# The last 96 gate and up columns as one token-major product, GpSimd's phi in quarters, another order of the first loads, and new due times

## The chip, the cores and the metric

The kernel runs on one core of one Trainium2 chip. Its metric is the device time in microseconds (us). A kernel's time is the median of its runs; a profile is one further look at a single execution.

## The reference

Two layers of the same kind are applied to a sequence x of 2048 tokens with 512 features, in bf16. Each layer has an attention part A and a gated part B, and both add to x:

```python
def A(x):                                    # x is layer-normed
    q, k, v = heads(x @ wqkv)                # 32 heads of 16
    pq, pk  = q @ w_phi[h], k @ w_phi[h]     # 16x16 for each head
    phi_q = concat(softmax(pq), softmax(-pq))
    phi_k = concat(softmax(pk), softmax(-pk))
    kv, z = phi_k.T @ v, sum(phi_k)          # over all tokens
    return ((phi_q @ kv) / (phi_q . z + 1e-6)) @ wo

def B(x):                                    # x is layer-normed
    gate, up = x @ W_gate, x @ W_up          # 512 -> 1376
    return (relu(gate) * up) @ W_down        # 1376 -> 512

x = x + A(norm(x)); x = x + B(norm(x)); x = x + A(norm(x)); x = x + B(norm(x))
```

The attention is linear: the sums kv and z over all tokens must be complete before the first query can be answered, in each layer.

## The kernel before

The 2048 tokens are 16 tiles of 128. All of x stays in SBUF (X, four chunks of four tiles). Weights are folded at the start: Wk2 and Wq2 are wk and wq times the block-diagonal form Wblk of w_phi (`fold`, line 500, fed by turned weights, line 492).

Each layer has these stages:

- **Keys** (`Keys.tile`), for each tile: K (line 555) and V (561) on TensorE; two exponentials ek on ScalarE (558); their sums over 16 features on VectorE (566); a logarithm and an exponential as a reciprocal on ScalarE (569, 571); the product phiK (575) on GpSimd in layer 0, on VectorE in layer 1 (the last tile of layer 0 and the last two of layer 1 are halved between both); and the sums kv and z (590) on TensorE, which accumulate in three PSUM banks.
- **Queries** (`queries`, 627 and 631), for a chunk of four tiles: Q on TensorE, then two exponentials Eq on ScalarE.
- **Attention** (`attend`), for each tile: Eq times R (645), where R is made of the finished sums (607, 614); ScalarE evacuates to N and DS (652); six VectorE operations up to o (658 to 670); a transpose to oT; wo (674); and the addition to X (678).
- **MLP** (`mlp`), for a block of one, two or four tiles (`BLOCKS`): statistics (524, 525), centring (693), a transpose to xnTB, gate and up (717), relu and copy on ScalarE (729, 732), their product hT on VectorE (735), down (753), and the addition to X (760), after which the next layer's norm of that tile, or its store, can begin.

In gate and up the weights are the stationary operand. The 1376 columns are ten groups of 128 and one of 96, and a group takes four matmuls for gate and four for up, each as wide as the block has tokens (128, 256 or 512). The result lies feature by feature, as down needs it. `step` groups share a PSUM bank in narrow blocks, and the group of 96 has its own evacuations and product.

Norms are transposed by TensorE (515, with ident) for some tiles at the start and at stage changes, else by a DMA transpose in SyncE's queue (512). SyncE also issues most loads (421) and the stores (814). Before the keys, SyncE loads x0, x1, w_phi (wf) and further x tiles; ScalarE issues four loads, wk and wv in halves, and then loads its table (435). wk lies in the first hT buffer at that time. Eight matmuls on zeros (472) start TensorE's clock.

The order of the work is settled before anything is emitted. Every instruction group is an `Op` with an engine, a cost and a due time. `plan` walks through time and lets, on each engine, the operation with the earliest due time go among those that can start; it knows buffers, a DMA queue with a rate, eight DMA lanes, and a flag `port` that keeps VectorE and GpSimd operations on a shared port apart. The due times are the table `DUE`, one number for each operation. The engines' programs then hold the instructions in that order, with the waits that the data need.

Of the kernel before, what the change touches and what calls it, by code (L numbers as in the profile page):

```python
# [8 lines left out]
P = 128  # L9
D = 512  # L10
H = 32
DH = 16
F = 1376
NB = D // P
NF = 11
T = 16
# [48 lines left out]
LANES = 8  # L65


def plan(ops):
# [14 lines left out]
    while len(order) < len(ops):  # L83
# [9 lines left out]
        for e, cand in open_.items():  # L93
# [14 lines left out]
            if first is None or (best is not None and first >= best[0]):  # L108
                continue
            best = first, min((o for t, o in at if t <= first + 1), key=rank)  # L110
        assert best is not None, "no instruction can go"
        t, o = best
# [5 lines left out]
        if o.move:  # L118
            queue = max(t + 1400, queue) + o.move
            lat = max(lat, queue + 600 - t)  # L120
            lanes = lanes[1:] + [t + lat + HOP["SP"]]
# [75 lines left out]
POOL_PHI = (1930, 1940)  # L197
# [8 lines left out]
class K:  # L206
# [8 lines left out]
PHI = ["POOL"] * 15 + ["BOTH"]  # L215
# [5 lines left out]
    12838, 22903, 21957, 14591, 13091, 13645, 15535, 64723, 20066, 21946, 22404, 37433, 28497, 23438, 37063, 39628,  # L221
    28785, 29551, 44842, 28330, 24305, 34896, 63622, 64383, 20084, 27070, 12367, 25403, 16122, 20963, 16400, 20414,
    28622, 14745, 13296, 0, 20852, 19738, 11034, 1902, 20892, 15574, 21335, 14487, 15440, 22432, 23645, 18853, 17105,
    22553, 28873, 19773, 26092, 25340, 25787, 23828, 13120, 23528, 21785, 24083, 23090, 21952, 20538, 24815, 23457,
    25970, 23550, 31010, 25099, 23275, 18650, 19003, 26038, 17503, 25082, 25647, 15810, 16800, 15591, 12341, 14834,
    14960, 22006, 26736, 27644, 31701, 20249, 19795, 19482, 28729, 28028, 25143, 23422, 23168, 21986, 20764, 21010,
    18380, 22535, 26069, 26704, 26760, 27662, 26937, 23439, 25716, 25111, 22983, 25319, 23584, 22831, 20905, 24972,
    20900, 23792, 31557, 26979, 24090, 26712, 27328, 29633, 36593, 23721, 21790, 27888, 29989, 28308, 24211, 23690,
    16282, 27043, 28746, 63959, 20753, 24108, 22204, 20506, 28938, 31501, 16952, 23241, 24872, 26922, 26823, 26681,
    23442, 21284, 21898, 21956, 23204, 34727, 23722, 25793, 25045, 24516, 28101, 34925, 27683, 29170, 28253, 28875,  # L230
    30193, 28228, 27230, 20124, 19920, 25218, 34824, 20364, 26494, 23600, 22279, 25188, 32338, 24418, 23597, 25625,
    24807, 22909, 26881, 23790, 23537, 27214, 30398, 27170, 29691, 24862, 29838, 30880, 31272, 31170, 24090, 19394,
    24355, 27559, 28096, 28185, 27041, 16432, 19783, 20871, 21413, 25680, 24329, 22590, 23232, 28648, 34644, 25165,
    27573, 28614, 28868, 26952, 25768, 33460, 18665, 20698, 17926, 25363, 24420, 41432, 26543, 26946, 21970, 28607,
    28989, 25096, 31074, 29971, 29937, 25959, 28788, 30567, 21366, 23689, 25468, 26088, 25065, 28026, 32472, 33442,
    31477, 34059, 28202, 31806, 26064, 29854, 28369, 27149, 33755, 29216, 28180, 39321, 29625, 29410, 29759, 29949,
    30883, 29890, 21203, 25098, 24304, 21581, 23455, 24475, 31469, 24994, 27083, 22812, 27946, 25205, 43875, 15559,
    25460, 23347, 27182, 23482, 28342, 27010, 22914, 29784, 25417, 28800, 29241, 25959, 25485, 27617, 28609, 37268,
    25605, 25139, 29044, 33664, 26596, 31241, 22317, 27365, 31505, 25855, 27240, 29739, 29776, 24515, 29496, 27055,
# [115 lines left out]
def kernel(  # L355
# [80 lines left out]
    for t in (2, 3):  # L436
        load_x(t, 1, 3 + t)
    for t in (4, 6):
        load_x(t, 2, 3 + t)
# [413 lines left out]
```

The softmax here doesn't subtract the row's maximum and nothing guards it: scores larger than these inputs give would overflow.

## Time and profile before

| | before |
|---|---|
| median of 5 runs | 399.43 us (398.39 to 400.02) |
| the profiled execution, its own time | 399.67 us |
| its span, from the first to the last instruction | 397.8 us |
| mean granted TensorE clock | 0.996 |
| TensorE (PE) busy | 385.9 us, 2819 matmuls |
| VectorE (DVE) busy | 267.4 us |
| ScalarE (ACT) busy | 258.9 us |
| GpSimd (POOL) busy | 34.2 us |

The span leaves 1.87 us of that execution outside. An engine's busy time is the union of its instructions. A matmul's duration in the profile runs from its start until its results have drained, and consecutive matmuls overlap, so the mean of one is longer than the time from one to the next. PEld are the weight loads, which run beside matmuls.

### The profile page before, as it was taken

What the parts mean: (1) busy time and instruction counts of PE and PEld (TensorE: products, weight loads), DVE (VectorE), ACT (ScalarE), POOL (GpSimd) and SP (SyncE); (2) the same over time, 40 slices, a digit from 0 to 9 for tenths busy, and PEclk for the clock granted to TensorE, in tenths of its full rate; (3) what the DMA queues carried; (4) which work ended last, traced back from release to release, by engine and by line L of the source; (5) the groups of instructions that cost most, each with busy time, mean ns of one, the idle gap of its engine ahead of it and who ended that gap; (6) DMA issues with size and microseconds to landing.
All of it is one profiled execution on the core that took longest, in us unless ns stands there. A gap on an engine that the chain in (4) does not pass through costs nothing.

```text
span 397.8 us, 7594 instructions
## 1 busy us (share of the span) xinstructions
PE 385.9 (97%) x2819; PEld 232.6 (58%) x2819; DVE 267.4 (67%) x657; ACT 258.9 (65%) x694; POOL 34.2 (9%) x24
## 2 busy tenths in 40 slices
PE   6998999999999999999999999999999999999996
PEld 4453555786664444454666755577865444444866
DVE  5999846999999442488882458699997513423323
ACT  4788999986835666536684569998842651660622
POOL 0255980000000000000000003000000000000000
PEclk9899999999999999999999999999999999999999
DMA  7457760125424100130100100013334102001010
GB/s 213 94 138 195 202 172 1 28 55 82 80 28 80 28 0 0 28 67 15 40 16 2 26 0 2 4 34 72 69 73 99 29 0 67 15 1 51 16 41 28
DMA packets 56293, 21.78 MB, mean 55 GB/s; under 512 B 48096, under 2 KB 55232, under 8 KB 56256
## 3 DMA queue, kind: packets, MB, share of 16 engines
q1 hardware_dynamic: 55168, 20.25, 22.8%
q10 hardware_dynamic: 1088, 1.05, 0.8%
q8 instruction: 22, 0.36, 0.4%
q14 instruction: 15, 0.12, 0.1%
HBM read 7.91 MB, written 2.10 MB: 25 GB/s over the span
## 4 chain that ended last, share of the span: by engine, by line
PE 74%; DVE 12%; ACT 4%; issue 2%; DVEq 0%
PE b L717 34%; PE b L753 17%; PE b L561 5%; PE b L555 5%; PE b L674 4%; PE b L627 4%; PE q L590 3%; DVE X L678 2%; ACT Eq L631 2%; DVE bstB L524 2%; DVE pr L667 2%; PE q L645 1%; DVE o L670 1%; ACT N L652 1%; DVE m L662 1%
## 5 line engine op out<-in xcount | busy, mean ns | idle before, releaser
L717 PE MATMUL b<-xnTB,wu 128*128 128x128 bf16 (+4 forms) x660 | 89.7, 279 | 0.1
L717 PE MATMUL b<-xnTB,wg 128*128 128x128 bf16 (+5 forms) x660 | 89.3, 279 | 0.0
L729 ACT ACTIVATE gu<-b 128x512 bf16<-128x512 f32 (+4 forms) x98 | 54.6, 572 | 51.4 <-PE b L717 51.1
L735 DVE TENSOR_TENSOR hT<-gu 128x512 bf16<-128x512 bf16 (+4 forms) x98 | 38.0, 393 | 71.2 <-ACT gu L732 70.8
L753 PE MATMUL b<-wd,hT 128*128 128x512 bf16 (+2 forms) x363 | 83.2, 373 | 0.0
L732 ACT CAST gu<-b 128x512 bf16<-128x512 f32 (+3 forms) x98 | 54.3, 563 | 37.6 <-PE b L717 36.9
L717 PEld LDWEIGHTS <-wu 128*128 128x128 bf16 (+1 forms) x660 | 55.2, 100 | 25.1 <-issue 0.4
L717 PEld LDWEIGHTS <-wg 128*128 128x128 bf16 (+1 forms) x660 | 55.0, 100 | 25.5
L753 PEld LDWEIGHTS <-hT 128*128 128x128 bf16 (+1 forms) x363 | 34.8, 98 | 34.8
L575 POOL TENSOR_TENSOR phiK<-ek,sk 128x1024 bf16<-128x1024 bf16 (+1 forms) x18 | 33.5, 1875 | 213.1 <-ACT sk L571 208.3
L652 ACT CAST N<-q 128x384 bf16<-128x384 f32 (+1 forms) x96 | 48.4, 593 | 2.8 <-PE q L645 2.5
L631 ACT ACTIVATE Eq<-b 128x512 bf16<-128x512 f32 x64 | 40.5, 676 | 7.5 <-PE b L627 7.4
L566 DVE TENSOR_REDUCE sk<-ek 128x64 f32<-128x1024 bf16 x32 | 38.2, 1212 | 10.5 <-ACT ek L558 10.1
L558 ACT ACTIVATE ek<-b 128x512 bf16<-128x512 f32 x64 | 35.7, 615 | 5.4 <-PE b L555 5.2
L760 DVE SCALAR_TENSOR_TENSOR X<-b,rsB,X 128x512 bf16<-128x512 f32 (+1 forms) x33 | 23.1, 727 | 23.2 <-PE b L753 23.2
L561 PE MATMUL b<-wv,xnTA 128*128 128x512 bf16 x128 | 33.2, 387 | 0.7 <-ACT ek L558 0.7
L555 PE MATMUL b<-Wk,xnTA 128*128 128x512 bf16 x128 | 32.4, 381 | 1.3 <-ACT vext L479 1.2
L674 PE MATMUL b<-wo,oT 128*128 128x512 bf16 x128 | 32.2, 379 | 1.4 <-ACT oT L479 0.8
L627 PE MATMUL b<-xnTA,Wq 128*128 128x512 bf16 x128 | 31.5, 379 | 0.3 <-ACT Eq L631 0.3
L652 ACT COPY DS<-q 128x48 f32<-128x48 f32 (+1 forms) x96 | 25.3, 344 | 3.1 <-PE q L645 2.2
L645 PE MATMUL q<-R,Eq 128*128 128x144 bf16 x256 | 25.4, 226 | 0.6 <-ACT N L652 0.6
L645 PEld LDWEIGHTS <-Eq 128*128 128x128 bf16 x256 | 19.2, 98 | 8.2 <-issue 0.9
(63 smaller groups left out, 375.2 us busy)
## 6 DMA issues: line engine op xcount, KB each, us to landing
out_dram<-X SPq DMA_DIRECT2D x15, 128.0 KB, 1.7
X<-in_A_x_dram SPq DMA_DIRECT2D x6, 256.0 KB, 3.5
wg<-in_B_W_gate_dram SPq DMA_DIRECT2D x4, 344.0 KB, 4.3
wu<-in_B_W_up_dram SPq DMA_DIRECT2D x4, 344.0 KB, 3.9
wd<-in_B_W_down_dram SPq DMA_DIRECT2D x5, 256.0 KB, 4.2
hT<-in_A_wqkv_dram ACTq DMA_DIRECT2D x2, 256.0 KB, 3.6
X<-in_A_x_dram SPq DMA_DIRECT2D x4, 128.0 KB, 3.7
wv<-in_A_wqkv_dram ACTq DMA_DIRECT2D x2, 256.0 KB, 4.6
```

What stands on the lines that cost most here:

```text
L555: k = op("PE", mm(4, 512), due, lambda: [nc.tensor.matmul(kp.t[:], lhsT=xnTA[c][:, b, cols], rhs=Wk2[:, b, :], start=(b == 0), stop=(b == ...
L561: v = op("PE", mm(4, 512), due_v, lambda: [nc.tensor.matmul(vp.t[:], lhsT=xnTA[c][:, b, cols], rhs=wv[:, b, :], start=(b == 0), stop=(b == ...
L566: a = op("DVE", SUM16, due, lambda: nc.vector.tensor_reduce(out=sk.t[:], in_=ek.t[:].rearrange("p s (h f) -> p (s h) f", f=DH), axis=AX.X, ...
L627: q = op("PE", mm(4, 512), due(c, b), lambda b=b, qp=qp: [nc.tensor.matmul(qp.t[:], lhsT=Wq2[:, m, b * P:(b + 1) * P], rhs=xnTA[c][:, m, : ...
L631: done.append(op("ACT", act(512), due(c, b), lambda b=b, s=s, qp=qp: nc.scalar.activation(out=Eq[c][:, b, s, :], in_=qp.t[:], func=AF.Exp, ...
L645: pe.append(op("PE", mm(len(groups), GE), due, lambda ps=ps, groups=groups: [nc.tensor.matmul(ps.t[:, n * GE:(n + 1) * GE], lhsT=Eq[c][:, ...
L652: nc.scalar.copy(out=q[:, k, 0:3] if k < 2 else q[:, :, 3], in_=ps.t[:, 0:n * GE].rearrange("p (n c j) -> p n c j", n=n, j=HB)[:, :, lo:hi])
L674: a = op("PE", mm(4, 512), due + 3, lambda: [nc.tensor.matmul(yp.t[:], lhsT=oT.t[:, b, :], rhs=wo[:, b, :], start=(b == 0), stop=(b == NB ...
L717: nc.tensor.matmul(ps.t[:m, q * W:(q + 1) * W], lhsT=w[:, b, g * P:g * P + m], rhs=xT.t[:, b, 0:W], start=(b == 0), stop=(b == NB - 1))
L729: nc.scalar.activation(out=gu.t[:m, 0, lo * W:hi * W], in_=gp.t[:m, lo * W:hi * W], func=AF.Relu)
L732: nc.scalar.copy(out=gu.t[:m, 1, lo * W:hi * W], in_=up.t[:m, lo * W:hi * W])
L753: nc.tensor.matmul(yp.t[:, 0:c1 - c0], lhsT=h.t[:m, f * W + i * P:f * W + (i + 1) * P], rhs=wd[:m, f, c0:c1], start=(f == 0), stop=(f == N ...
```

## The change

The change has four parts.

1. **Gate and up.** wg and wu become one tile, wgu. The last 96 columns of both are computed together with xT as the stationary operand: for each tile of tokens four matmuls with 192 moving columns (96 of gate, 96 of up), so that the result lies token by token. Two tiles share a PSUM bank. ScalarE takes relu of the gate half into gr, VectorE multiplies by the up half from PSUM into hr, whose last 32 columns of each tile are zeroed once at the start, and one DMA transpose for each block on SyncE's queue brings hr into hT's last group. The ten groups of 128 stay as they were.
2. **phi.** GpSimd's 64 heads (two signs of 32) of a tile become four instructions of 16 heads; where GpSimd has half a tile, two.
3. **First loads.** ScalarE issues two loads (x0, the second half of wk) and then its table load. SyncE issues the first half of wk, wf, both halves of wv, and then x1 to x7. The zeros for the first matmuls are written first on VectorE.
4. **The planner.** A tie between engines goes to the one that has waited longer, the DMA queue is taken as faster at its start, and all due times are new (one for each operation of the new list).

```diff
+FR = F - (NF - 1) * P
+FRESH = 0.77
...
-            if first is None or (best is not None and first >= best[0]):
+            if first is None or (best is not None and first > best[0]):
                 continue
-            best = first, min((o for t, o in at if t <= first + 1), key=rank)
+            o = min((o for t, o in at if t <= first + 1), key=rank)
+            came = max(clock[e], o.ready)
+            if best is None or first < best[0] or came < best[1]:
+                best = first, came, o
...
-            queue = max(t + 1400, queue) + o.move
+            queue = max(t + 1400, queue) + o.move * (FRESH if queue < 9000 else 1.0)
...
-PHI = ["POOL"] * 15 + ["BOTH"]
+PHI = dict(POOL=[("POOL", 16)] * 4, DVE=[("DVE", 64)], BOTH=[("DVE", 32), ("POOL", 16), ("POOL", 16)])
+PHI0 = ["POOL"] * 15 + ["BOTH"]
...
-    wg, wu, wd = new("wg", [NB, F]), new("wu", [NB, F]), new("wd", [NF, D])
+    wgu, wd = new("wgu", [2, NB, F]), new("wd", [NF, D])
...
+    p_gr, p_hr = pool("gr", 2, [2, FR]), pool("hr", 2, [4, P])
...
-    load_x(0, 1, 0)
-    l_wv = [load(0, wv[:, b:b + 2, :], wqkv[:, b:b + 2, 2 * D:3 * D], 262144, "ACT") for b in (0, 2)]
-    load_x(1, 1, 1)
-    l_wk = [load(1, wk[:, b:b + 2, :], wqkv[:, b:b + 2, D:2 * D], 262144, "ACT") for b in (0, 2)]
...
+    a0, a1, _ = chain([first_x(0, 1, "ACT"), w_load(wk, 1, 2, "ACT"), lambda f: op(
+        "ACT", (1300, 1300), 5, lambda: nc.scalar.preload_act_table_set("natural_log_exp_and_others"), name="tbl",
+        follow=f)])
+    b0, l_wf, b1, b2, *_ = chain([
+        w_load(wk, 1, 0, "SP"),
+        lambda f: load(2, wf[:], A_w_phi.rearrange("(b j) d f -> (j d) b f", b=NB, j=8), 65536, "SP", f),
+        w_load(wv, 2, 0, "SP"), w_load(wv, 2, 2, "SP"), first_x(1, 1), first_x(2, 1), first_x(3, 1), first_x(4, 2),
+        first_x(6, 2)])
+    l_wk, l_wv = [b0, a1], [b1, b2]
...
+    hr_zero = [op("DVE", dve(4 * (P - FR), 4), 9000, (lambda v: lambda: nc.vector.memset(v[:, :, FR:P], 0.0))(v),
+                  name="hr0", port=True) for v in p_hr.tiles]
...
+            for e, n in PHI[phi_eng]:
+                q, cost = (nc.vector, dve(n * DH)) if e == "DVE" else (nc.gpsimd, (POOL_HEAD * n, POOL_HEAD * n + 10))
+                parts.append(op(e, cost, due, lambda q=q, lo=lo, n=n: phi(q, lo, n), [a], [] if lo else [ph],
+                                [ek, sk] + ([ph] if lo else []), name="phi", port=True))
+                lo += n
...
+        for i0 in range(0, n, 2):
+            k = min(2, n - i0)
+            ps, gr = Buf(p_b), Buf(p_gr)
+            def both(ps=ps, i0=i0, k=k):
+                for q in range(k):
+                    for b in range(NB):
+                        nc.tensor.matmul(ps.t[:, q * 2 * FR:(q + 1) * 2 * FR],
+                                         lhsT=xT.t[:, b, (i0 + q) * P:(i0 + q + 1) * P],
+                                         rhs=wgu[:, :, b, F - FR:F], start=(b == 0), stop=(b == NB - 1))
...
+            a = op("PE", mm(4 * k, 2 * FR), due_g(0), both, turned + l_wg + l_wu, [ps], [xT], name="GU")
+            a = op("ACT", act(k * FR), due_g(0), relu, [a], [gr], [ps], name="rr")
+            tails.append(op("DVE", dve(k * FR), due_g(0), times, [a] + hr_zero, [] if i0 else [hr],
+                            [gr, ps] + ([hr] if i0 else []), name="hr"))
-        for f0 in range(0, NF, step):
+        for f0 in range(0, NF - 1, step):
...
+        made[NF - 1] = op("SP", (340 + 215 * n, XPOSE[1]), due_g(0), lambda: nc.sync.dma_start_transpose(
+            out=h.t[:, (NF - 1) * W:NF * W].rearrange("p (i t) -> p i t", t=P),
+            in_=hr.t[:, 0:n, :].rearrange("p i f -> p (i f)")), tails, (), [hr, h], name="hrT", move=125 * n)
```

## The prediction

> **What bounds the kernel now.** I read the page's head first, then a table of windows cut where TensorE (PE) changes from waiting to full, then the groups by form, then the timeline of the start.
>
> ```profile
> PE 385.9 (97%) x2819; PEld 232.6 (58%) x2819; DVE 267.4 (67%) x657; ACT 258.9 (65%) x694; POOL 34.2 (9%) x24
> ```
>
> PE is busy 385.9 of 397.8 us, so everything that is not PE work is 11.9 us. The windows say where (columns: busy us of PE, PEld, DVE, ACT, POOL, granted clock, DMA share, GB/s):
>
> ```profile
> 0.00:12.00 12.00, 8.71 (x53) 5.02 (x54) 6.99 (x21) 5.08 (x11) 0.70 (x6) 0.87 0.63 187
> 12.00:40.00 28.00, 25.14 (x160) 12.78 (x159) 27.31 (x50) 23.95 (x75) 13.31 (x7) 0.99 0.59 150
> 62.00:72.00 10.00, 8.70 (x75) 5.41 (x74) 6.95 (x25) 10.00 (x36) 0.00 (x0) 1.00 0.00 1
> 72.00:116.00 44.00, 44.00 (x439) 31.82 (x437) 43.93 (x132) 34.39 (x117) 0.00 (x0) 1.00 0.35 59
> 116.00:248.00 132.00, 131.93 (x799) 73.77 (x798) 83.80 (x166) 80.85 (x186) 2.99 (x2) 1.00 0.12 24
> 248.00:262.00 14.00, 12.65 (x104) 7.50 (x103) 10.25 (x34) 13.78 (x46) 0.00 (x0) 1.00 0.07 11
> 392.00:398.00 6.00, 2.75 (x32) 2.28 (x29) 1.81 (x5) 0.88 (x3) 0.00 (x0) 1.00 0.08 23
> ```
>
> PE idles 3.29 us to 12 us (much of that stretch at half clock), 2.86 us from 12 to 40 us, 1.30 and 1.35 us at the two changes from keys to attention, where ACT is full (10.00 and 13.78), and 3.25 us in the tail. From 72 to 248 us and from 262 to 392 us it has no gap: a column less there is time less, and 72 to 116 us is as full on DVE (43.93 of 44). From 12 to 40 us DVE (27.31 of 28) and ACT are the limit, not PE.
>
> **What the change cuts on PE.** The groups by form:
>
> ```profile
> L717 PE MATMUL b<-xnTB,wg 128*96 128x512 bf16 x16 | 4.1, 379 | 0.0
> L717 PE MATMUL b<-xnTB,wg 128*96 128x256 bf16 x20 | 3.0, 273 | 0.0
> L717 PE MATMUL b<-xnTB,wg 128*96 128x128 bf16 x24 | 2.3, 219 | 0.0
> ```
>
> The eleventh group fills 96 of 128 array columns and costs as much as a full one (379 ns, as the 128-wide form). wu has the same three rows. These means hold the drain; the spacing comes from the chain of waits, where 16 matmuls of 128 columns take 0.89 us, 8 of 256 take 0.87 and 4 of 512 take 0.86: 55.6, 109 and 216 ns. The Trainium skill, "TensorE: Matmul & The Clock Gate", section "Wait — 56ns, not 53.3ns?", gives N/2.4 + 2.5 ns for warm start-to-start; the trace agrees. For the new 192 columns, which no row shows, that is an estimated 82.5 ns. In place of 8 matmuls of a block's width come 4 of 192 for each tile:
> - six one-tile blocks: 8 x 55.6 less 4 x 82.5 = 115 ns each, 0.69 us;
> - five two-tile blocks: 8 x 109 less 8 x 82.5 = 212 ns, 1.06 us;
> - four four-tile blocks: 8 x 216 less 16 x 82.5 = 408 ns, 1.63 us.
>
> **Sum -3.4 us**, all inside full PE stretches. Bounds -3.7 to -1.2, for a pitch of 80 to 100 ns over 128 matmuls (a weight load takes 98 ns, but at a pitch of 55.6 it already overlaps). The new order has 2827 matmuls for 2819: 120 go, 128 come.
>
> **What that costs elsewhere.** ACT drops 30 evacuations of 96 partitions (2.4 + 1.9 + 1.9 relu, 2.3 + 1.9 + 2.0 copy = 12.4 us) for 13 relus of 192 and 6 of 96 elements at some 0.36 and 0.32 us: -5.8 us, worth nothing under a full PE. DVE drops 15 products (4.3 us) and gets 19 from PSUM, at 0.35 and 0.25 us (R, 128x256 from PSUM, takes 0.42): +1.8 us, of which about 0.6 falls in 72 to 116 us where DVE is full. SP gets 15 transposes (2.4 us from issue to landing in the page's DMA rows, 1.2 us of SP each at most). In SP's new order the first stands ahead of oT, so a late product would hold attention's transposes. SP has about 22 transposes of 1.25 us in those 44 us, so there is room, and the new product comes early in each block while its reader, the last third of down, is the block's end. The new product needs all eight gate and up loads, issued by 41 us; the first block starts at 74. The two hr memsets stand on DVE while it waits for x. Taken: +0.2 us; bounds 0 to +2.
>
> **The first loads.**
>
> ```profile
> 0.73 0.99 ACTq L421 DMA_DIRECT2D hT<-in_A_wqkv_dram  x2
> 1.75 2.57 ACTq L421 DMA_DIRECT2D wv<-in_A_wqkv_dram  x2
> 4.35 1.28 ACT L435 ACT_TABLE_LOAD   x1 [4.35 <-DMA hT<-in_A_wqkv_dram]
> 6.21 0.41 DVE L535 TENSOR_SCALAR xn<-X,mvA,rsA 128x512 bf16<-128x512 bf16 x1 [2.14 <-ACT rsA L532]
> 7.82 0.66 DVE L464 TENSOR_TENSOR Wblk<-wf,Mf 128x512 bf16<-128x512 bf16 x1
> 8.53 1.51 PE L500 MATMUL b<-Wblk,hT 128*128 128x128 bf16 x16 [1.46 <-DVE Wblk L464]
> ```
>
> ACT issues four loads before the table load, which ends at 5.63; ln waited for it although the statistics were done at 4.06. After, ACT issues two: x0 and half of wk, so the table can end by about 3.3 and xn start at 4.06 + 0.03 + 0.33 + 0.24 = about 4.7 instead of 6.21. Wblk follows xn directly in the new DVE order and no longer waits behind a statistic and a copy; with wf second in SP's queue it may run at 5.1 to 5.8, then two copies of hT (if wf lands late, these and the fold stand behind it). The fold can begin at 6.7 (after the last turn) instead of 8.53, and the first K at about 10.2 instead of 11.98: 1.8 us. Some is given back: x1 to x3 now stand behind wv on SP; DVE reaches their xn only after six further operations at about 12.3, so K of tile 1 comes near 13.5, where it now starts by 12.9, and PE waits there. By tile 2 (17.29 now, some 15.2 then) the lead is back, since wv is done. **Taken -1.7 us**, bounds 0 and -2.5. The half-clock stretch makes this the least certain term: the same skill page, "What's actually happening", says that about 3.4 us of sustained activity free the clock; here the gaps at 6.2 and 7.1 us kept it low to about 12 us, and the new order has fewer of them.
>
> **GpSimd in quarters.**
>
> ```profile
> L535 DVE TENSOR_SCALAR xn<-X,mvA,rsA 128x512 bf16<-128x512 bf16 x16 | 10.4, 678 | 2.1 <-ACT rsA L532 2.1
> L575 POOL TENSOR_TENSOR phiK<-ek,sk 128x1024 bf16<-128x1024 bf16 x15 | 29.0, 1948 | 27.9 <-ACT sk L571 23.1 <-PE b L627 2.5 <-PE q L590 1.8
> L575 POOL TENSOR_TENSOR phiK<-ek,sk 128x512 bf16<-128x512 bf16 x3 | 4.5, 1510 | 185.1 <-ACT sk L571 185.1
> ```
>
> The median of those 16 is 407 ns and the longest 2029: 10.4 less 16 x 0.407 leaves 3.9 us that DVE stands while a phi runs. "SBUF — State Buffer", section "SBUF: two separate sides", says that DVE and GpSimd take a shared port pair as an exclusive lock for a whole instruction; 2029 ns against 407 agrees. The timeline has the waits at 25.2, 29.9 and 43.3 us; behind the first two ACT then stands 1.12 and 1.61 us for mvA, and PE 0.5 us for ek and 1.2 us for vext, before 30.35 and 33.47 us. With quarters a wait is at most one quarter, so some 2.5 of the 3.9 us on DVE go, and of PE's 2.86 idle us about 1.6 go; what is late next is ACT, full from 35 to 60 us. **Taken -1.6 us**, bounds -3 and +1. The upper bound is the price of a start: no row shows a quarter. In proportion to 1948 ns it is 487 ns. "GPSIMD Engine Reference", section 3.1, tells of two software dispatch hops in an instruction without a number for this case. The half at 1510 ns overlaps a DVE phi and is no clean price.
>
> **Due times.** Everything moves in the order, and both key-to-attention gaps (2.65 us together) stay set by ACT, with about as many Q products left to fill them (24 and 28 matmuls before, 20 and 32 after the last sums). Taken 0, bounds -1.2 and +1.5, since a full stretch can only lose. The tail ends in the same chain (11 halves of down, product, store): 0.
>
> **Sum**: -3.4 + 0.2 - 1.7 - 1.6 = -6.5 us. The profiled execution took 399.67 us for a span of 397.8; I expect 391.3 and 393.2. It stands 0.24 above the median of 399.43, so the forecast in terms of the median is **392.9 us**.
>
> **Rivals.**
> 1. *Only the PE columns count* (0.18). DVE's and ACT's work before 60 us is unchanged, and PE is full from 42 us on; late x1 to x3 eat the start. Speaks for it: ACT is full from 35 us whatever DVE does. Against: PE can take up the earlier work, since it idles 2.86 us from 12 to 40. 399.4 - 3.4 + 0.2 = 396.2 us.
> 2. *All of the gaps go* (0.10): the bounds -2.5 and -3 and 1 us of the due times. 399.4 - 3.2 - 5.5 - 1 = 389.7 us.
> 3. *GpSimd becomes the bound, slower* (0.04). It must finish 15 tiles between about 15.5 and 56 us: 60 quarters, 675 ns each. Above that the last sums slip. At 850 ns they slip by 10 us, of which the other gains (6.5) take back most: 403 us. The decisive point for slower is 675 + (6.5 / 60) = 785 ns, 300 ns over proportion. Against: the page has 28 us of GpSimd idle, and nothing in the trace shows a start so dear.
> 4. *The columns are not cheaper* (0.03): at a pitch of 109 ns instead of 82.5 the cut is gone (26.5 ns x 128 = 3.4 us), for instance if the pair of gate and up slices streams slower than one run; the rest stays, 396.3 us. Against: the 128-column products, with as many weight loads, run at 55.6.
>
> The main case has 0.65, with 390.9 to 394.9 of its own. The range takes in rival 1 and most of 2. A difference of 0.3% (1.2 us) is about what a measurement of this kernel can tell from no change.
>
> **What would show it.** Right: 128 matmuls of 192 columns with a mean near 248 ns (82.5 + the drain of 166), none waiting; the table load done before 3.5 us; fold before 7.2; xn's longest under 0.95 us; PE busy near 382; no PE gap from 70 to 245. Wrong: POOL's quarters over 600 ns; a wait of PE for hr or hT's transpose; PE idle over 6 us before 40 us; DVE holding PE between 70 and 112 us.

## The result and the profile after

| | before | after |
|---|---|---|
| median | 399.42 us, 47 runs (398.31 to 400.30) | 396.63 us, 26 runs (393.41 to 399.98) |
| profiled execution, its own time | 399.67 us | 398.42 us |
| its span | 397.8 us | 396.6 us |
| mean granted TensorE clock in it | 0.996 | 0.991 |
| PE busy, matmuls | 385.9 us, 2819 | 384.2 us, 2827 |

The ratio is 0.9934, with a 95% interval from 0.9923 to 0.9945: 2.8 us faster, where the forecast was 6.5 us faster, 392.9 us, with a main case up to 394.9. One thing is needed to read the numbers below: in some executions a stretch of the first 20 us runs at half clock, and the mean granted clock of an execution tells it. In the profile of before that stretch goes from 8.98 to 12.40 us (3.41 us, mean clock 0.996), in the profile of after from 12.04 to 18.87 us (6.83 us, mean clock 0.991); the number 0.50 is the granted clock:

```profile
8.98:12.40 3.42, 3.42 (x21) 2.02 (x18) 2.54 (x6) 1.66 (x3) 0.00 (x0) 0.50 0.17 38
```

```profile
12.04:18.87 6.83, 6.09 (x24) 2.66 (x21) 6.00 (x11) 3.68 (x11) 2.35 (x4) 0.50 0.47 127
```

An execution with a mean of 0.999 or 1.000 is said below to have the full clock. The kernel before took 398.34 us in such executions and about 399.5 where the mean was 0.995 or 0.996, each about half of its runs. Of the changed kernel's runs only five had the full clock (median 394.85 us); the others have a median of 396.77 us.

The page's head of the changed kernel, then its table of windows, cut as before (busy us of PE, PEld, DVE, ACT, POOL, granted clock, DMA share, GB/s):

```profile
PE 384.2 (97%) x2827; PEld 231.9 (58%) x2827; DVE 270.4 (68%) x663; ACT 257.0 (65%) x683; POOL 40.6 (10%) x72
```

```profile
0.00:12.00 12.00, 8.80 (x60) 4.58 (x60) 8.70 (x30) 7.05 (x16) 0.70 (x6) 1.00 0.76 209
12.00:40.00 28.00, 26.35 (x160) 13.48 (x157) 25.01 (x45) 23.92 (x75) 17.83 (x31) 0.88 0.61 132
40.00:62.00 22.00, 21.14 (x157) 12.16 (x158) 11.02 (x13) 19.66 (x53) 19.16 (x32) 1.00 0.61 177
72.00:116.00 44.00, 43.83 (x426) 31.69 (x425) 37.14 (x114) 31.03 (x95) 0.00 (x0) 1.00 0.29 56
116.00:248.00 132.00, 131.85 (x839) 74.64 (x838) 96.33 (x194) 84.25 (x207) 2.96 (x4) 1.00 0.15 29
262.00:392.00 130.00, 128.36 (x1000) 80.79 (x998) 72.34 (x208) 67.46 (x167) 0.00 (x0) 1.00 0.23 47
```

The stretch from 12 to 40 us looks fuller on PE than before (26.35 against 25.14 us), but its clock is 0.88: busy time that is half-speed time. From 72 to 248 us PE is full but for 0.32 us, as forecast. From 262 to 392 us it idles 1.64 us, where before it had no gap.

The groups by form show the columns' and GpSimd's parts (busy us, mean ns, then the idle time of the engine before them):

```profile
L823 PE MATMUL b<-wgu,xnTB 128*128 128x192 bf16 x128 | 13.3, 246 | 0.1
L832 DVE TENSOR_TENSOR hr<-gr,b 128x192 bf16<-128x192 bf16 x13 | 4.2, 339 | 3.0 <-ACT gr L828 3.0
L683 POOL TENSOR_TENSOR phiK<-ek,sk 128x256 bf16<-128x256 bf16 x66 | 39.9, 639 | 203.7 <-ACT sk L679 198.1 <-PE b L669 3.9 <-PE b L736 0.8
```

The 192-column matmul takes 246 ns with its drain, where the forecast had 248, and nothing waits ahead of it. A quarter of phi takes 639 ns, not 487. The table of waits of PE (us in total, number of times, longest) has a kind of releaser that it did not have before, a DMA. In the changed kernel's lines L663 is K, L669 V, L736 Q, L783 wo, L881 down, L608 the fold, L623 the transposes of a norm on TensorE, L620 a DMA transpose and L868 that of hr.

```profile
PE b L783 <- DMA oT<-o: 1.6, 2, 1.0
PE b L736 <- DMA xnTA<-xn: 1.5, 1, 1.5
PE b L623 <- DVE xn L643: 1.3, 1, 1.3
...
PE b L663 <- ACT xnTA L587: 0.7, 1, 0.7
```

The timelines of the start (ACT, then DVE, then PE, each with its start and duration in us and, in brackets, the idle time before it):

```profile
1.68 1.28 ACT L537 ACT_TABLE_LOAD   x1 [1.68 <-PEq L965]
...
5.46 0.69 DVE L573 TENSOR_TENSOR Wblk<-wf,Mf 128x512 bf16<-128x512 bf16 x1
...
6.21 0.38 PE L608 MATMUL b<-Wblk,hT 128*128 128x128 bf16 x4
...
8.36 0.59 PE L663 MATMUL b<-Wk,xnTA 128*128 128x512 bf16 x2
...
11.50 0.76 PE L623 MATMUL b<-ident,xn 128*128 128x128 bf16 x8 [1.33 <-DVE xn L643]
13.00 1.89 PE L663 MATMUL b<-Wk,xnTA 128*128 128x512 bf16 x4 [0.74 <-ACT xnTA L587]
```

The table is loaded by 2.96 us, the fold starts at 6.21 us and the first K at 8.36, 1.8 us ahead of the forecast's 10.2 (two of its four matmuls; the last of the four ends at 10.17). Then PE waits twice, for the norms of the later tiles. The next K, that of the third tile, takes 1.89 us for four matmuls, where four at full clock take 1.03: the clock has fallen to half.

### The profile page after: what moved, and what is told of

It is laid out like the page before. It is cut to its first block, busy times and chain, and to the rows that moved or that the text cites. A ratio compares the mean times of both kernels' runs of the same rounds, so it can differ in the third digit from the quotient of the medians.

```text
span 396.6 us, 7656 instructions
## 1 busy us (share of the span) xinstructions
PE 384.2 (97%) x2827; PEld 231.9 (58%) x2827; DVE 270.4 (68%) x663; ACT 257.0 (65%) x683; POOL 40.6 (10%) x72
## 4 chain that ended last, share of the span: by engine, by line
PE 82%; ACT 7%; DMA 5%; DVE 4%; issue 1%; DVEq 0%
PE b L847 33%; PE b L881 18%; PE b L663 6%; PE b L669 6%; PE b L783 6%; PE b L736 4%; PE q L699 3%; DMA oT<-o 3%; PE b L823 3%; PE q L754 2%; ACT Eq L740 2%; ACT N L761 2%; DMA xnTA<-xn 1%; ACT DS L761 1%; ACT ek L666 1%
## 5 line engine op out<-in xcount | busy, mean ns | idle before, releaser
L847 PE MATMUL b<-xnTB,wgu 128*128 128x128 bf16 (+2 forms) x1200 | 152.1, 279 | 0.1
L847 PEld LDWEIGHTS <-wgu 128*128 128x128 bf16 x1200 | 98.0, 98 | 45.9 <-issue 0.3
L881 PE MATMUL b<-wd,hT 128*128 128x512 bf16 (+2 forms) x363 | 85.2, 373 | 0.0
L851 ACT ACTIVATE gu<-b 128x512 bf16<-128x512 f32 x83 | 49.9, 605 | 39.1 <-PE b L847 39.1
L854 ACT CAST gu<-b 128x512 bf16<-128x512 f32 (+1 forms) x83 | 48.8, 590 | 36.3 <-PE b L847 35.8
L857 DVE TENSOR_TENSOR hT<-gu 128x512 bf16<-128x512 bf16 (+1 forms) x83 | 33.9, 410 | 43.0 <-ACT gu L854 42.7
L683 POOL TENSOR_TENSOR phiK<-ek,sk 128x256 bf16<-128x256 bf16 x66 | 39.9, 639 | 203.7 <-ACT sk L679 198.1
L881 PEld LDWEIGHTS <-hT 128*128 128x128 bf16 (+1 forms) x363 | 34.3, 98 | 31.2 <-DVE hT L857 0.4
L761 ACT CAST N<-q 128x384 bf16<-128x384 f32 (+1 forms) x96 | 44.6, 534 | 5.0 <-PE q L754 3.9
L663 PE MATMUL b<-Wk,xnTA 128*128 128x512 bf16 x128 | 34.4, 394 | 1.4 <-ACT xnTA L587 0.7
L783 PE MATMUL b<-wo,oT 128*128 128x512 bf16 x128 | 32.7, 379 | 2.8 <-DMA oT<-o 1.6
L669 PE MATMUL b<-wv,xnTA 128*128 128x512 bf16 x128 | 33.1, 387 | 0.0
L736 PE MATMUL b<-xnTA,Wq 128*128 128x512 bf16 x128 | 31.4, 379 | 1.5 <-DMA xnTA<-xn 1.5
L787 DVE TENSOR_TENSOR X<-X,b 128x512 bf16<-128x512 bf16 x32 | 21.7, 677 | 6.3 <-PE b L783 6.0
L761 ACT COPY DS<-q 128x48 f32<-128x48 f32 (+1 forms) x96 | 20.3, 278 | 6.1 <-PE q L754 3.8
L632 DVE BATCH_NORM_STATS2 bstA<-X 128x6 f32<-128x512 bf16 x32 | 21.4, 686 | 2.1 <-DMA X<-in_A_x_dram 1.8
```

The lines of the kernel that those rows point to most:

```text
L663: k = op("PE", mm(4, 512), due, lambda: [nc.tensor.matmul(kp.t[:], lhsT=xnTA[c][:, b, cols], rhs=Wk2[:, b, :], start=(b == 0), stop=(b == ...
L669: v = op("PE", mm(4, 512), due_v, lambda: [nc.tensor.matmul(vp.t[:], lhsT=xnTA[c][:, b, cols], rhs=wv[:, b, :], start=(b == 0), stop=(b == ...
L683: e.tensor_tensor(out=ph.t[:].rearrange("p s (h f) -> p (s h) f", f=DH)[:, lo:lo + n], in0=ek.t[:].rearrange("p s (h f) -> p (s h) f", f=D ...
L736: q = op("PE", mm(4, 512), due(c, b), lambda b=b, qp=qp: [nc.tensor.matmul(qp.t[:], lhsT=Wq2[:, m, b * P:(b + 1) * P], rhs=xnTA[c][:, m, : ...
L761: nc.scalar.copy(out=q[:, k, 0:3] if k < 2 else q[:, :, 3], in_=ps.t[:, 0:n * GE].rearrange("p (n c j) -> p n c j", n=n, j=HB)[:, :, lo:hi])
L783: a = op("PE", mm(4, 512), due + 3, lambda: [nc.tensor.matmul(yp.t[:], lhsT=oT.t[:, b, :], rhs=wo[:, b, :], start=(b == 0), stop=(b == NB ...
```

## The experiments

Labels beginning with e are runs; all ratios are to the kernel before, measured on the same chip; the runs were on three chips, on which before at full clock agrees within 0.1 us. The theory was: the columns work as costed, and what is missing went to (a) the half clock behind the new gap at 10 to 13 us, (b) transposes in SyncE's queue that land late, because hr's transposes take turns there and because PE's instruction fetches share a DMA engine with them. The first rival was that the columns themselves are worth less; the second, that quarters cost what they free.

**e1_filled_gap.** Eight matmuls on zeros in the gap, in the changed kernel:

```diff
         for o in order:
+            if o.n in (107, 89):        # 5 ahead of the next two norms' transposes, 3 ahead of the next K
+                for _ in range({107: 5, 89: 3}[o.n]):
+                    nc.tensor.matmul(wps.t[:], lhsT=p_h.tiles[0][:, 0:P], rhs=p_h.tiles[0][:, 0:512], start=True, stop=True)
             o.emit()
```

> The changed kernel with eight dummy matmuls of 512 columns on zeros in TensorE's early gap: five ahead of the transposes that wait for xn, three ahead of the next K. Nothing is left out. Clock theory: the gaps at 9.8 to 13.0 us let the clock fall to half from 13.4 to 18.7 us, which costs 2 to 2.9 us in the profiled execution; with the gap filled the matmuls of 12 to 19 us run at full clock, the granted clock in the window from 12 to 40 us is over 0.97 instead of 0.88, and the median falls from 396.6 to 394 to 395.3. Rival, the early clock does not matter because VectorE and ScalarE limit that stage anyway: the clock rises and the median stays within 396 to 397.2. Rival, instruction fetches alone make the loss: no change, and the same waits for transposes later.

Measured 395.60 us (395.34 to 396.09), ratio 0.9914 [0.9899, 0.9930], clock 0.999 or 1.000 in each of six runs. Windows from 12 to 20 us, of after and of this run:

```profile
12.00:20.00 8.00, 7.26 (x32) 3.31 (x30) 6.04 (x11) 4.61 (x13) 2.35 (x4) 0.57 0.41 112
```

```profile
12.00:20.00 8.00, 7.81 (x57) 4.24 (x56) 8.00 (x14) 7.32 (x25) 4.65 (x8) 1.00 0.43 110
```

In the same 8 us 57 matmuls (at most three of the added ones among them) pass for 32. Work added to PE made the kernel 1.0 us faster in the median and narrowed its spread from 6.6 us (26 runs) to 0.75 us (six). Shown: without the gap the clock stays full. It does so in all 35 executions of the seven versions with the eight matmuls (e1, e9 to e14), against only five of the changed kernel's own. What the clock alone is worth is less sure: the changed kernel's own five full-clock runs lie 1.9 us below the others, e5's three 2.5 us. Filling the gap brings 1.0 us net; why not the whole is open. This run is the base for the later ones.

**e6_norms_first.** The other way at the gap: the norms of the next tiles ahead of other DVE and ACT work from 8 to 13 us.

```diff
+    after(82, 83)                       # after(n, x, ...): put operations x behind n in the order
+    after(39, 84, 85, 104)
+    after(41, 103)
+    after(103, 104, 105, 86, 106)
+    after(50, 87, 107, 88, 89)
```

> The changed kernel with the order of VectorE and ScalarE from 8 to 13 us altered: the aggregate, logarithm, exponential and xn of tile 2 run before the statistics of tiles 4 and 1, its transpose first on TensorE, its xnTA before the second ek on ScalarE. Nothing is left out. Clock and gap theory: TensorE's wait before 11.5 us shrinks from 1.3 to under 0.5 us and the next K starts near 11.5 instead of 13.0 us; whether or not the clock then holds, the median falls by 0.8 to 2 us, to 394.6 to 395.8. Rival, the stage is limited by VectorE and ScalarE and gives the lead back by 40 us: 396 to 397.

Measured 396.07 us (395.65 to 396.65), 0.9929 [0.9912, 0.9947], again the full clock in all six runs. But the transpose of the second tile's norm then waits 1.9 us for xn:

```profile
14.60 0.40 PE L623 MATMUL b<-ident,xn 128*128 128x128 bf16 x4 [1.89 <-DVE xn L643]
```

The clock is won and half of what e1 gained goes into the wait that was only moved. And a single gap of 1.89 us did not cost the clock here.

**e2_feature_major.** The last 96 columns back as features on the partitions, in the places of the new products; hr's transposes go, a DVE product writes hT.

```diff
-            for q in range(k): ... lhsT=xT.t[:, b, (i0 + q) * P:(i0 + q + 1) * P], rhs=wgu[:, :, b, F - FR:F]
+            for s, c in parts: ... lhsT=wgu[:, s, b, F - FR:F], rhs=xT.t[:, b, 0:W]
-        made[NF - 1] = op("SP", ..., nc.sync.dma_start_transpose(... hr ...))
+        made[NF - 1] = op("SP", ..., nc.vector.tensor_tensor(... h, z[:FR, 0, 0:W], z[:FR, 1, 0:W] ...))
```

> The changed kernel with the last 96 columns of gate and up computed feature by feature again (15 blocks, 120 matmuls of the block's width, a relu, a copy and a product, no transpose of hr), at the same places in the order as the token-major product. Columns theory: TensorE gets its 3.4 us back, the median rises from 396.6 to 399 to 400.5. Rival, the added transposes in SyncE's queue cost as much as the columns save: the median stays at 396 to 397.5. Rival, the columns are not cheaper at all: 394.5 to 396.5, since the transposes go. In every case 2819 matmuls.

Measured 398.06 us (395.94 to 399.37, 22 runs), 0.9969 [0.9957, 0.9982]. The change's columns are worth 1.4 us as they stand, not 3.4. PE's waits for oT by DMA are gone, its wait for xnTA (1.4 us) is not. This run mixes full and half clocks (six of 22 runs were at full clock); e14 repeats it at full clock.

**e5_no_hr_transpose.** hr's transposes left out; the last group of down reads a constant block, so the last 96 gate columns' own values are missing from the output.

```diff
-            lambda: nc.sync.dma_start_transpose(out=h.t[...], in_=hr.t[...])
+            lambda: None
-            lhsT=h.t[:m, f * W + i * P:f * W + (i + 1) * P]
+            lhsT=(h.t[...] if f < NF - 1 else ident[:m, :])
```

> The changed kernel without the 15 DMA transposes of hr; down's eleventh group reads the identity matrix in their place, so the last 96 of the 1376 products are left out of the output. All else is as in the changed kernel, the token-major product included. Queue theory: each transpose holds SyncE for 1.1 to 1.2 us however small it is (the planner reckons 0.555 us for one tile), the oT behind them start later, and a fetch of instructions that meets them does the rest; without them the waits of TensorE for oT (1.6 and 2.1 us in two profiles) go, and the median falls from 396.6 to 394.4 to 395.6, which with the 1.4 us that the token-major product is worth as it stands comes near the 3.4 us of its columns. Rival, the columns are worth 1.4 us only and the transposes nothing: 396.2 to 397.

Measured 394.19 us (392.73 to 395.81), 0.9881 [0.9853, 0.9908]. No wait for oT by DMA. Three runs had the full clock (392.73 to 393.25 us), three did not (395.14 to 395.81).

**e3_fetch_shifted.** The first eight matmuls of 512 columns become 32 of 128 (same time), so that PE's later instruction fetches come at other places of its work (in the trace's DMA records the ones at 38.4, 276.9 and 308.8 us come at 34.1, 273.0 and 304.1).

```diff
-        wps.t[:], lhsT=..., rhs=p_h.tiles[0][:, 0:512] ...) for _ in range(8)]
+        wps.t[:, 0:P], lhsT=..., rhs=p_h.tiles[0][:, 0:P] ...) for _ in range(32)]
```

> The changed kernel with its eight first matmuls of 512 columns cut into 32 of 128, so that TensorE has 48 instructions more ahead of all the others and the same 3.4 us of warming. Nothing is left out. Fetch theory: TensorE's instructions come in pieces of 16 KB, each holds one DMA engine for about 1 us, and the waits of TensorE for DMA transposes at 38.8, 277.9 and 311.5 us of the changed kernel (1.5, 1.0 and 0.6 us) are the transposes that such a fetch met; with the fetches 48 instructions earlier these three waits go or move to other transposes, and fetches stand some 3 to 10 us earlier in the trace. The median moves by up to 2 us in either direction. Rival, the transposes are late because SyncE issues too many in a row: the three waits stay where they are, at the same length.

Measured 396.37 us (395.04 to 396.63), 0.9922 [0.9902, 0.9942]. Three lines of its waits:

```profile
PE b L663 <- DMA xnTA<-xn: 1.9, 1, 1.9
PE b L623 <- DVE xn L643: 1.3, 1, 1.3
...
PE b L783 <- DMA oT<-o: 0.2, 1, 0.2
```

The wait for oT falls from 1.6 to 0.2 us, with hr's transposes in their old places; the wait for xnTA moves to the K before it and grows. So a fetch in the same moment is part of what makes these transposes late (one profile each; in five other profiles with hr's transposes in their old places, those of after, e1, e6, e7 and e9, the waits for oT are 1.0 to 2.1 us). The DMA queues of the changed kernel from 276 to 279 us, where PE waits for oT:

```profile
q1 hardware_dynamic: 544, 0.13, 23.0%
q8 instruction: 1, 0.02, 2.2%
```

2.2% of 16 engines for 3 us is 1.06 us of one engine for one piece of instructions; from 280 to 290 us, where oT is on time, there is no such line.

**e8_sync_order.** Three moves on SyncE in the changed kernel: xnTA of one tile ahead of a load, two hr transposes behind oT. The first move put that transpose ahead of the normalisation that feeds it, so it turned the buffer's earlier content, and it was no test of the first move.

```diff
+    after(250, 189)
+    after(1569, 1741)
+    after(1659, 1901)
```

> The changed kernel with three moves in SyncE's queue alone: the transpose of xn on which TensorE waits near 39 us goes ahead of the two loads before it (x of two tiles, one slice of gate), and the two transposes of hr that stand ahead of oT near 274 and 306 us go behind it. Nothing is left out. Queue and fetch theory: these transposes then land before or beside the fetch, TensorE's waits for DMA (1.5, 1.0 and 0.6 us in the changed kernel's profile) fall under 1 us together, the median falls from 396.6 to 394 to 395.5. Rival, a fetch delays any transpose in flight, and with the work earlier it only meets another one: 396 to 397, with waits for DMA of over 2 us in the profile.

Measured 397.96 us (397.30 to 401.03, 14 runs), 0.9984 [0.9968, 1.0000]: a new wait of V for vext (1.8 us), and down waits 0.8 us for hr. Inconclusive; e9 to e11 do it properly.

**e9_xnta_early.** e1, and that transpose directly behind its normalisation, ahead of two loads:

```diff
+    after(188, 189)
```

> The changed kernel with the eight matmuls in the start's gaps, and the transpose of the third normalisation (xnTA, L620) issued ahead of the two loads that stand before it in SP's order. Nothing is left out. If the wait of Q for xnTA near 39 us (1.3 us in the kernel with the filled gaps) is the issue order's doing, it goes and the time is 395.6 - 1.3 = about 394.3 us. If the engine that holds the last part of the transpose is what delays it (instruction fetches), or the loads moved back become late instead, a wait of 1 us or more stays between 30 and 45 us and the time stays within 0.4 us of 395.6. If that wait was cover for later work, it goes and the time stays at 395.6.

Measured 394.56 us (394.49 to 394.78), 0.9887 [0.9870, 0.9904]: the wait of Q (1.3 us in e1) is gone, and 1.04 us with it. (The text calls it the third normalisation; it is that of a tile near 30 us.)

**e10_hr_after_ot.** e1, with `after(1569, 1741)` and `after(1659, 1901)`.

> The changed kernel with the eight matmuls in the start's gaps, and two of the fifteen transposes of hr (L868, the ones near 270 and 302 us) issued on SP behind the transpose of o that they stood ahead of. Nothing is left out. Theory: hr's transposes hold SP's queue 1.2 us each and push oT late; then the waits of proj for oT by DMA (2.1 us together in the kernel with the filled gaps) go, and the time is 395.6 - 2 = about 393.6 us. Rival, the oT transposes are late because an instruction fetch shares their DMA engine: the waits stay at 1.5 us or more and the time is 395.6. Rival, the down projection needs hr's transpose so early that its wait takes the place: a wait of down for hT of 1 us or more, time 395 to 396.

Measured 394.91 us (393.87 to 396.09), 0.9895 [0.9877, 0.9914]. PE near 276 us, in e1 and here:

```profile
276.23 0.82 PE L783 MATMUL b<-wo,oT 128*128 128x512 bf16 x3 [1.29 <-DMA oT<-o]
```

```profile
275.99 0.39 PE L881 MATMUL b<-wd,hT 96*128 96x512 bf16 x1 [1.00 <-DMA hT<-hr]
276.22 0.81 PE L783 MATMUL b<-wo,oT 128*128 128x512 bf16 x3
```

The third rival of its text, at this place: whichever of the two goes second in SyncE's queue is what PE waits for, and wo starts at the same 276.2 us. The whole run is 0.7 us below e1 in the median, with a spread of 2.2 us: at the second place, near 309 us, the wait for oT (0.81 us in e1) is gone.

**e11_both_orders.** e9 and e10's second move.

> The changed kernel with the eight matmuls in the start's gaps, xnTA ahead of its two loads as in the run before, and of the hr transposes only the one near 302 us behind its oT. Nothing is left out. If the waits add and SP's order sets them: 395.6 - 1.3 - 1.0 = about 393.3 us. If instruction fetches set them: 395.6. One in between (394.3) says that only one of the two is the order's.

Measured 394.53 us (394.00 to 395.32), 0.9886 [0.9869, 0.9903], the same as e9, whose wait at the second place was only 0.32 us. So the gains of the two moves don't add. The fastest version here that leaves nothing out is e9 with its equal e11, about 2 us faster than the changed kernel.

**e12_gap_no_hr** is e1 with e5's edit, **e13_all_waits_off** adds `after(188, 189)`. Both leave the last 96 gate columns' values out.

> The changed kernel with the eight matmuls in the start's gaps and without the fifteen transposes of hr: the last group of the down projection reads a constant block instead, which leaves out the last 96 gate columns' own values from the output; every matmul stays. If the low clock of the start and the hr transposes are two separate losses that add up, 395.6 - 1.5 to 2 = 393.6 to 394.1 us, and every run within 0.5 us of the others. If leaving out the transposes only gained by the clock that its runs happened to get, the time is 395.6. If even more is lost to the transposes than the waits show, below 393.3.

> The changed kernel with the eight matmuls in the start's gaps, xnTA ahead of its two loads, and without the fifteen transposes of hr (the last group of the down projection reads a constant block, which leaves out the last 96 gate columns' own values; every matmul stays). If the three losses found so far are what the prediction lacked, they add: 396.6 - 1.0 (clock) - 1.0 (xnTA) - 2.1 (hr) = 392.5 us, near the 392.9 of the forecast. If the two transposes' losses are one and the same (a shared delay that moves), 393.5 us as without the hr transposes alone.

Measured 393.49 us (393.25 to 393.80), 0.9862 [0.9842, 0.9882], and 392.94 us (392.64 to 393.21), 0.9859 [0.9838, 0.9879]. hr's transposes (with all waits for what they bring) cost 2.1 us on e1 and 1.6 us on e9; xnTA's place costs 1.0 us with them and 0.55 without, so about 0.5 us of the two losses is shared.

**e14_columns_undone** is e9 with e2's edit: the columns' price at full clock.

> The changed kernel with the eight matmuls in the start's gaps and xnTA ahead of its two loads, with the last 96 gate and up columns back as features on the partitions (block-wide matmuls, no transpose of hr), in the places of the new products. Nothing is left out. The base is 394.56 us. If the token-major columns cut 3.4 us of PE work and give 2.1 of it back through the hr transposes, undoing both gives 394.6 + 1.3 = about 395.9 us. If the columns are worth all of 3.4 us, 398.0. If they are worth nothing, 394.6.

Measured 396.20 us (395.80 to 396.81), 0.9939 [0.9924, 0.9954]. e13, which has the new products without their transposes, is 3.26 us faster than this; e9, which has both, 1.64 us.

**e4_before_quarters.** The kernel before with phi on GpSimd in quarters, nothing else.

```diff
+            def quarters(s, n):
+                for lo in range(s * H, (s + n) * H, 16):
+                    nc.gpsimd.tensor_tensor(out=v[0][:, lo:lo + 16], in0=v[1][:, lo:lo + 16], in1=sk... )
-                a = [op("POOL", POOL_PHI, due, lambda: phi(nc.gpsimd, 0, 2), ...
+                a = [op("POOL", POOL_PHI, due, lambda: quarters(0, 2), ...
```

> The kernel before with GpSimd's phi in quarters of 16 heads and nothing else changed (same order on every engine). Port theory as in the prediction: VectorE's xn in layer 0 lose their 3.9 us of waiting but for about 1 us, TensorE's gaps from 28 to 37 us shrink, the time falls by 0.5 to 2 us to 397.4 to 399. Rival, a quarter costs 640 ns instead of 487 as in the changed kernel, so that a tile takes 2.5 us instead of 1.95 and GpSimd, which had few gaps from 38 to 57 us, becomes late at the end of the keys: the time stays or rises by up to 4 us (399.4 to 403).

Measured 397.19 us (397.01 to 397.41), 0.9953 [0.9938, 0.9968], at 643 ns for a quarter. GpSimd does not become the bound.

**e7_whole_phi.** The changed kernel with the quarters joined again: one instruction of 64 heads in the first quarter's place (32 in a half tile), nothing in the others.

> The changed kernel with GpSimd's phi as one instruction of 64 heads again (32 where it has half a tile), at the place of the first quarter. Nothing is left out. If quarters are worth in the new order what they were worth in the old (1.9 us there), the median rises from 396.6 to 397.8 to 399.5 and VectorE's longest xn is near 2 us again. Rival, the due times of the new order were made for quarters that end early and a whole phi of 1.95 us instead of 4 x 0.64 = 2.56 gives the last sums back 0.6 us a tile: 395.5 to 397.

Measured 397.80 us (395.23 to 399.24, 13 runs), 0.9964 [0.9947, 0.9980]: the quarters are worth 1.2 us in the medians of the new order too (0.7 us between the full-clock runs, of which this one has two).

**e15_before_loads** and **e16_loads_dve_order.** The kernel before with the first loads alone (the zeros for the first matmuls stay where they were).

```diff
+    first = [by[n] for n in (0, 5, 7, 4, 6, 1, 2, 3, 8, 9, 10, 11)]   # x0, wk, table | wk, wf, wv, wv, x1 ...
+    order = first + [o for o in order if o not in first]
+    ...                                 # Wblk (20) behind the first xn (44)
+    for n in (57, 58, 59, 60): ...      # e16 only: the second tile's statistics behind the copies of hT (27)
```

> The kernel before with the first loads alone in the new order: ACT issues the first tile of x, half of wk and the table load, SP the other half of wk, wf, both halves of wv and the rest of x; Wblk directly behind the first normalisation on DVE. Nothing is left out. The prediction's step gives 399.4 - 1.7 = 397.7 us. If the late x tiles eat the earlier fold, 399.4, with PE waits for the norms of tiles 1 to 3 near 12 to 16 us. If the start is worth nothing because the stretch to 40 us is set by ACT and DVE, 399.4 without such waits.

> The kernel before with the first loads in the new order as in the run before, and the statistics of the second tile behind the two copies of hT on DVE, so that a late x no longer holds the fold. Nothing is left out. The prediction's step (fold before 7.2 us, first K 1.8 us earlier, 1.7 us of it kept) gives 397.7 us. If an earlier first K is absorbed before 40 us because DVE (full there) and the late tiles of x decide, the fold is early and the time still 399.2 to 399.5. Something between, 398.5, says that half of the lead is kept.

e15 measured 399.35 us (398.20 to 401.28, 22 runs), 1.0007 [0.9995, 1.0019]. The statistics of the second tile waited 1.77 us on DVE for an x that now comes late, the copies of hT stood behind them, and the fold waited 2.0 us. e16 measured 398.15 us (397.55 to 398.57, 14 runs), 0.9990 [0.9982, 0.9998] against runs of before of which 15 in 19 had the full clock. Its windows (those of before stand in the prediction) and its first K:

```profile
0.00:12.00 12.00, 9.16 (x58) 4.96 (x60) 8.39 (x24) 6.21 (x13) 0.70 (x6) 1.00 0.65 198
12.00:40.00 28.00, 25.09 (x164) 13.11 (x165) 27.59 (x49) 24.70 (x80) 14.68 (x8) 1.00 0.65 165
```

```profile
10.11 1.02 PE L556 MATMUL b<-Wk,xnTA 128*128 128x512 bf16 x3
```

The first K comes at 10.11 us for 11.98, just as forecast, and the profiled execution is 398.10 for 399.67 us. But the stretch before 12 us is at clock 1.00 for 0.87: most of the lead is the half clock that is gone. How much shows in e4, which up to the first phi is the kernel before, in an execution at full clock:

```profile
10.55 1.03 PE L555 MATMUL b<-Wk,xnTA 128*128 128x512 bf16 x3
```

At full clock the loads bring the fold from 8.56 to 7.18 us, but the first K from 10.55 to 10.11 only: statistics and norm of the second tile, whose x now comes later, stand from 7.64 us on among the copies of the folded weights that K reads. All 14 runs have the full clock, and against before's full-clock runs (398.34 us) only 0.2 us is left.

**e17_loads_and_quarters.** e16 and e4 together.

> The run of this call without quarters, with phi on GpSimd in quarters as well. Nothing is left out. Quarters alone gave 397.19 us on the kernel before. If the lead of the first loads can be kept once DVE is freed from the waits, 397.2 - 1.7 = 395.5 us; if it is absorbed all the same, 397.2; if the two gains are the same idle time, 397.2 or more.

Measured 397.16 us (397.07 to 397.50), 0.9966 [0.9955, 0.9978], no less than quarters alone. In its profile PE's waits for vext (1.2 us) and ek (0.8 us), which e16 still has, are gone; three short waits for phi (0.5 us in all) are new.

## Why the prediction was wrong

The medians of the runs make a chain from before to after, in which each step is one part:

| from, to | what it adds | us | forecast |
|---|---|---|---|
| before 399.42, e16 398.15 | first loads (e16's runs all had the full clock, half of before's) | -1.3 | -1.7 |
| e16, e17 397.16 | quarters | -1.0 | -1.6 |
| e17, e14 396.20 | the new order, gap filled and xnTA early | -1.0 | 0 |
| e14, e13 392.94 | the columns on PE | -3.3 | -3.4 |
| e13, e9 394.56 | hr's transposes | +1.6 | +0.2 |
| e9, e1 395.60 | xnTA behind two loads | +1.0 | 0 |
| e1, after 396.63 | half clock behind the gap, net of filling it | +1.0 | 0 |

The forecast of 392.9 us is what e13 measures, in which the last three lines are taken away. A median here stands for within about 0.3 us, so the terms are good to about 0.4. That the total of the first four lines (-6.5 us) comes near the forecast's (-6.7 us) is partly luck: the loads and the quarters brought 1.0 us less and the order 1.0 us more.

- **Columns on PE: right.** In the timeline of PE sixteen of the new matmuls, of which the last takes 246 ns, stand in one row:

```profile
110.73 1.48 PE L823 MATMUL b<-wgu,xnTB 128*128 128x192 bf16 x16
```

1.48 less 0.246, over 15, is a pitch of 82 ns, as estimated, and the runs give 3.3 of 3.4 us. Rival 4 (columns not cheaper) falls.
- **What the columns cost elsewhere: the step that failed first.** "SP has about 22 transposes of 1.25 us in those 44 us, so there is room" counted room over a stretch; what counts is one moment. In the changed kernel o was ready near 273.4 us, and SyncE did this:

```profile
272.53 1.21 SPq L620 DMA_TRANSPOSE xnTB<-xn  x1
273.84 1.18 SPq L868 DMA_TRANSPOSE hT<-hr  x1
275.11 4.20 SPq L620 DMA_TRANSPOSE oT<-o  x2
```

oT's issue waits for hr's, and it meets a fetch: it has landed only when wo starts, at 279.34 us, 4.2 us after its issue, where the median is 2.4, and PE has idled 1.02 us. The prediction named the mechanism ("a late product would hold attention's transposes") and its bound of +2 about holds it; the value taken, +0.2, was mis-sized: it measures 1.6. And it looked at 72 to 116 us, while PE's two waits for oT lie near 279 and 312 us. And "its reader, the last third of down, is the block's end" was not enough cover: when hr's transpose goes second, e10 shows PE waiting 1.00 us for it.
- **First loads: wrong in what they are worth besides the clock.** In e16 the fold (7.18 us) and the first K (10.11) come about when forecast. But their gain was read against a profiled execution at half clock from 8.98 to 12.40 us, so it held about 1.15 us that only such executions lose. At full clock the fold gains 1.4 us, the first K 0.44 us and the kernel 0.2 us. Rival 1's "late x1 to x3 eat the start" was right about this part. Nor did the two early gaps alone keep the clock low, as the prediction has it: e4 waits 1.40 us for Wblk at the same place and has the full clock.
- **Quarters: right in the mechanism, 0.5 to 0.6 us too large.** xn's longest fell from 2029 to 887 ns as forecast, and with quarters PE's waits for vext and ek go, as e17 shows. A quarter costs 639 ns, above the 600 named as a sign against it, and PE's new waits for phi (0.5 us) take about what is missing. At full clock it is worth 1.15 us on the kernel before (398.34 to 397.19). e4 (quarters) and e16 (loads) both had the full clock in all of their runs, so in the medians that gain is counted once, not twice. Neither is shown to cause it: e15, with the same loads, had it in nine of 22 runs, before had it in 15 of 19 beside e16, and quarters begin near 16 us, behind the stretch. Rival 3 (GpSimd as the bound) falls.
- **Due times: not 0.** The new order brought 1.0 us and lost 1.0 by a transpose put behind two loads and 1.0 by the gap at 10 to 13 us. Bounded by -1.2 and +1.5 for both signs together, it holds; but two distinct risks were put in one term at 0. A wait there was foreseen ("K of tile 1 comes near 13.5"; the K that PE waits for comes at 13.0, but it is the third tile's, and that of the second comes at 19.14). Its effect on the clock was not: the prediction said that the new order "has fewer" of the gaps that keep the clock low.

The Trainium skill, "TensorE: Matmul & The Clock Gate", section "HAM oscillation — how this bites in real kernels", has the rule to leave no idle gap over about 3.4 us. Here no gap was as long: when the clock fell in the profile of after, at 12.04 us, the longest gap just before was 1.33 us, and with the gaps filled none of 35 executions lost the clock. But the length of one gap does not decide it either: e6 had one of 1.89 us at full clock, and five runs of the changed kernel itself kept the full clock. What decides between executions is not shown here.

The measured median is 0.4 us above rival 1's 396.2, which the range took in, but its story (only the columns count) isn't what happened: quarters, columns and order worked in their direction, the loads hardly at full clock, and the hr transposes, one late transpose and the clock gave 3.6 us back.

## What to carry to other kernels

A gain read off one profile must be split by the granted clock first: a part that also removes a half-clock stretch is worth its full lead only against executions that have one. For a transfer that a change adds to a queue, list what is ready in that queue at that moment and who waits for it, rather than the queue's free time over a stage. And a short idle gap of PE early in the kernel can be worth filling with matmuls on zeros (1.0 us here, and a narrower spread).

## What the runs showed of the hardware

- A DMA transpose takes about 1.2 us of SyncE's queue whatever its size, 1107 to 2082 ns with a median of 1182 for hr's blocks of one to four tiles, and lands some 2.4 us after its issue (up to 5.3 us between 28 and 42 us, where loads run beside it); the planner's cost for one tile of hr was 555 ns.
- One piece of PE's instructions holds one DMA engine for about 1.06 us (2.2% of 16 engines in 3 us); a transpose that meets it can land 1 to 2 us late, and 48 more instructions at the start move the place where that happens.
- Four GpSimd quarters of 128x256 took 4 x 639 = 2556 ns where one whole phi took 1948: some 200 ns for each of the three instructions more.
- The half-clock stretches lasted 3.41 us (before) and 6.83 us (after), and with the same instructions some executions have one and others none.
